# A decode-attention kernel: both output projections moved behind the last V, score chunks of 64 keys, q broadcast from its transpose

## The chip, the core and the metric

The kernel runs on one core of one Trainium2 chip. The metric is device time in microseconds, from several executions per kernel, each compared with executions of the kernel before on the same chip. All executions quoted here are of the state "fast". A time is a median; a "ratio" is the mean time of one kernel's fast runs over that of the other's fast runs of the same rounds, so it is not quite the ratio of two medians. The profile's "span" is shorter than the time, by about 1.8 us in nearly all executions. The 95% interval of every ratio is about 0.0013 either way, 3.4 us; where the text reads a smaller difference, it rests on the ranges of four or five runs each, and the kernel before stays within 0.4 us from one set of rounds to the next (medians 2583.15 to 2583.55).

## The reference

Two independent problems, A and B, each with batch 8, one query token, model width 1024, 32 heads of 128, and a cache of 4096 keys:

```
q      = x @ wq                                # [8, 32, 1, 128]
p      = softmax(q . k_cache * 128**-0.5)      # over 4096 keys
o      = p @ v_cache
result = o (heads side by side) @ wo           # [8, 1, 1024]
output = concat(A's result, B's result)        # bf16
```

K and V of one problem are 256 MiB each. Everything is bf16 and each cached value is used once, so the work is loading.

## The kernel before

The heads are taken eight at a time: a tile is 8 heads of one batch entry, 16 partitions per head, 256 keys per partition, 64 KB a partition, 8.39 MB. There are 64 K tiles and 64 V tiles, plus wq and wo of A and B, 8.39 MB each. SBUF has three slots of this size; K tiles alternate between slots 0 and 1, V has slot 2. One SyncE queue issues the loads in program order, each as soon as the last user of its slot has finished.

```python
put("wq", 0, 1); put("k", 0); put("wq", 1, 2)
for n in range(NQ - 1):                       # NQ = 64
    early = ...                               # some K in two halves
    put("k", n + 1, ...)
    put("v", n, 2)
    for c in range(NC):
        if n == done_at(c, NC, HB, B) + 1:    # wo of A in mid-program, 3/4 of wo of B late
            put("wo", c)
            late[n + 2] = c
put("v", NQ - 1, cuts=...)                    # last V in four pieces,
put("wo_last", 0, 2)                          # last quarter of wo of B among them
```

wo of A is loaded with contiguous rows of 64 KB a partition. wo of B is laid out by head, so that most of it can be projected before the last heads are done; its rows are 2 KB:

```python
opT[(kind, n)] = dma(to[:, 0:cols].rearrange("p (h n) -> p h n", n=D),
    caches[-1][4][heads.start * Dh:heads.stop * Dh, :].rearrange("(h p) n -> p h n", p=128), key, [dep])
```

For each K tile, in chunks of CT = 32 keys a partition, VectorE multiplies K by q in place and folds the 128 products to 64; TensorE adds four groups with the identity matrix; VectorE reduces the 16 left. After a whole tile come the maximum, the exponential (ScalarE), the masked weights PM (VectorE), and PV: 64 matmuls on TensorE, run while the next K tile is being scored. The end of PV frees the V slot. q is broadcast to the partitions of its head by eight small matmuls per tile.

```python
v, v * qbc                                   # make_mul,  VectorE
v[:, :, 0:64] + v[:, :, 64:128]              # make_fold, VectorE
matmul(dst, ident, v[:, :, j, :]) x 4        # make_eacc, TensorE
tensor_reduce(s_sb[...], red_ps[...], add)   # make_red,  VectorE
```

A small recorder in the file (class `_Program`) collects the operations of each engine and places the semaphore waits; every operation is emitted as straight code.

## Time and profile before

| | before |
|---|---|
| time | 2583.62 us (2583.49 to 2583.98, 3 runs) |
| span of the profiled execution | 2580.7 us |
| loaded | 1107.32 MB |
| VectorE busy | 2221.8 us, 86% |

The first lines are from the page of the kernel before: the busy time of each engine (share of the span, number of instructions), the loads' rate in 40 equal slices, the DMA queues (packets, MB, share of the time of 16 engines), and the chain of waits followed back from the end.

```profile
PE 1219.7 (47%) x7768; PEld 374.6 (15%) x7768; DVE 2221.8 (86%) x1809; ACT 105.2 (4%) x273; POOL 5.7 (0%) x23
GB/s 422 437 426 435 435 431 431 436 429 435 433 430 435 434 430 426 435 435 433 428 430 427 435 430 434 436 426 435 434 430 428 432 436 428 429 411 434 427 429 369
q1 hardware_dynamic: 23920, 1107.32, 99.5%
q8 instruction: 60, 0.98, 0.2%
q14 instruction: 18, 0.15, 0.0%
DMA 51%; DVE 46%; PE 2%; issue 1%; SPq 0%; ACT 0%; DVEq 0%
```

The queue of the loads (q1) is busy 99.5% of the time of 16 engines, at 430 GB/s nearly throughout. The chain of waits gives VectorE 46%, but that is how a chain is counted that walks through whatever released a load. A transfer that was released early and then stands behind another in the queue has not been delayed by its release: V is issued 8.1 us (median) before the last part of the load ahead of it lands.

Next, groups of instructions by line (operation, tiles and shapes, count, busy us, mean ns, idle time before and what ended it):

```profile
L305 DVE TENSOR_TENSOR ring<-ring,qbc 128x4096 bf16<-128x4096 bf16 x512 | 1169.0, 2283 | 327.0 <-DMA ring<-in_A_k_cache_dram 164.3
L310 DVE TENSOR_TENSOR ring<-ring 128x2048 bf16<-128x2048 bf16 x512 | 618.2, 1207 | 0.1
L327 DVE TENSOR_REDUCE s_sb<-red 128x32 f32<-128x512 f32 x512 | 348.3, 680 | 1.4 <-PE red L319 1.4
```

The multiply (L305) waits 327 us for K: VectorE is ahead of the loads. The table by stretch shows where the loads are slower than usual (stretch, length, busy us and instructions of PE, weight loads, VectorE, ScalarE, GpSimd, then TensorE's clock, DMA share, GB/s):

```profile
40.00:2280.00 2240.00, 1070.87 (x6720) 325.58 (x6720) 1975.59 (x1601) 87.66 (x233) 0.00 (x0) 0.60 1.00 432
2280.00:2340.00 60.00, 22.18 (x205) 8.17 (x206) 35.65 (x31) 1.48 (x4) 0.00 (x0) 0.61 0.99 405
2540.00:2575.00 35.00, 23.21 (x172) 9.77 (x172) 25.27 (x23) 1.20 (x3) 0.00 (x0) 0.63 0.89 371
```

The end of the chain of waits, in order of time (start, us, what):

```profile
2575.37 0.61 ACT accS L367
2576.02 0.28 PE o L384 x4
2576.39 0.45 DVE on_sb L420
2576.88 1.08 PE proj L439 x32
2577.98 0.42 DVE orow L447
```

After the last piece of V, the copy, the extraction of heads, the normalisation, a quarter of the projection and the store follow one another: about 6 us that nothing hides.

### The profile page before, as it was taken

The numbers are of one execution on the slowest core, as the hardware profiler recorded it, in microseconds if no ns is written. First come the engines' busy times: TensorE is split into PE (matmuls) and PEld (weight loads), VectorE is DVE, ScalarE is ACT, GpSimd is POOL, SyncE is SP. The second block draws the span as 40 slices with busy tenths as digits, with TensorE's granted clock in tenths as the row PEclk, the third lists the DMA queues.
The fourth block names the chain that finished last, engine by engine and source line by source line (L and its number), as shares of the span: only waits on it lengthen the run. The fifth ranks groups of instructions, "written<-read, shape, count | busy, mean of one in ns | idle before, by whom it ended". The sixth has DMA issues, their size and how long they took to land.

```text
span 2580.7 us, 17905 instructions
## 1 busy us (share of the span) xinstructions
PE 1219.7 (47%) x7768; PEld 374.6 (15%) x7768; DVE 2221.8 (86%) x1809; ACT 105.2 (4%) x273; POOL 5.7 (0%) x23
## 2 busy tenths in 40 slices
PE   2454454453554454454553445445345445453445
PEld 0111111111111111111111111111112111110112
DVE  3898898898898898898895889889889889887897
ACT  1100000000000000000000000000000000000000
POOL 0000000000000000000000000000000000000000
PEclk7665655655656655656655566565565565565656
DMA  9999999999999999999999999999999999999998
GB/s 422 437 426 435 435 431 431 436 429 435 433 430 435 434 430 426 435 435 433 428 430 427 435 430 434 436 426 435 434 430 428 432 436 428 429 411 434 427 429 369
DMA packets 24094, 1108.50 MB, mean 430 GB/s; under 512 B 2304, under 2 KB 2368, under 8 KB 6480
## 3 DMA queue, kind: packets, MB, share of 16 engines
q1 hardware_dynamic: 23920, 1107.32, 99.5%
q8 instruction: 60, 0.98, 0.2%
q14 instruction: 18, 0.15, 0.0%
q10 hardware_dynamic: 96, 0.05, 0.0%
HBM read 1107.33 MB, written 0.03 MB: 429 GB/s over the span
## 4 chain that ended last, share of the span: by engine, by line
DMA 51%; DVE 46%; PE 2%; issue 1%; SPq 0%; ACT 0%; DVEq 0%
DMA ring<-in_A_k_cache_dram 26%; DMA ring<-in_B_k_cache_dram 24%; DVE ring L305 24%; DVE ring L310 12%; DVE s_sb L327 6%; DVE PM L347 3%; PE red L319 2%; DVE rmax L333 1%; DMA ring<-in_B_v_cache_dram 1%; DVE rtmp L335 0%; DVE ngm L338 0%; PE pv L359 0%; SPq L158 0%; DVE rl L407 0%; DVE on_sb L414 0%
## 5 line engine op out<-in xcount | busy, mean ns | idle before, releaser
L319 PE MATMUL red<-ring,ident 128*128 128x512 bf16 x2048 | 836.5, 554 | 1321.2 <-DVE ring L310 1320.9
L305 DVE TENSOR_TENSOR ring<-ring,qbc 128x4096 bf16<-128x4096 bf16 x512 | 1169.0, 2283 | 327.0 <-DMA ring<-in_A_k_cache_dram 164.3
L310 DVE TENSOR_TENSOR ring<-ring 128x2048 bf16<-128x2048 bf16 x512 | 618.2, 1207 | 0.1
L319 PEld LDWEIGHTS red<-ring,ident 128*128 128x128 bf16 x2048 | 202.4, 120 | 1859.4 <-DVE ring L310 1590.8
L327 DVE TENSOR_REDUCE s_sb<-red 128x32 f32<-128x512 f32 x512 | 348.3, 680 | 1.4 <-PE red L319 1.4
L359 PE MATMUL pv<-ring,PM 128*32 128x512 bf16 x4096 | 320.2, 468 | 1.3 <-DMA ring<-in_B_v_cache_dram 1.3
L347 DVE TENSOR_TENSOR PM<-pe,own_h 128x2048 bf16<-128x2048 bf16 x64 | 146.2, 2284 | 0.7 <-ACT pe L341 0.7
L359 PEld LDWEIGHTS pv<-ring,PM 128*32 128x32 bf16 x4096 | 113.2, 113 | 216.1 <-issue 164.3
L341 ACT ACTIVATE pe<-s_sb,ngm 128x256 bf16<-128x256 f32 x64 | 32.5, 508 | 1008.0 <-DVE ngm L338 1008.0
L367 ACT ACTIVATE accS<-pv 128x512 bf16<-128x512 f32 x64 | 38.2, 597 | 846.0 <-PE pv L359 846.0
L295 ACT ACTIVATE qbc<-misc 128x128 bf16<-128x128 f32 x64 | 17.8, 278 | 580.6 <-PE misc L290 580.6
L333 DVE TENSOR_REDUCE rmax<-s_sb 128x1 f32<-128x256 f32 x64 | 26.9, 420 | 2.2
L290 PE MATMUL misc<-q_sb,selb 8*32 8x128 bf16 x512 | 26.2, 295 | 1.5 <-ACT q_sb L278 1.5
L377 PE MATMUL o<-accS,E 128*32 128x32 bf16 x512 | 18.1, 177 | 0.0
L335 DVE TENSOR_SCALAR rtmp<-half,rmax 128x32 f32<-128x32 f32 x64 | 15.4, 241 | 2.2
L290 PEld LDWEIGHTS misc<-q_sb,selb 8*32 8x32 bf16 x512 | 9.2, 103 | 54.7 <-issue 54.7
L377 PEld LDWEIGHTS o<-accS,E 128*32 128x32 bf16 x512 | 14.8, 94 | 13.6 <-ACT accS L367 8.1
L439 PE MATMUL proj<-ring,on_sb 128*8 128x256 bf16 x256 | 12.1, 372 | 9.4 <-DMA ring<-in_A_wo_dram 5.8
L338 DVE TRANSPOSE_TENSOR_REDUCE ngm<-rtmp 128x1 f32<-128x32 f32 x64 | 13.5, 211 | 2.2
L399 PEld LDWEIGHTS o<-rsum,own_m 128*128 128x128 f32 x64 | 14.5, 333 | 4.4 <-ACT pe L341 3.3
L399 PE MATMUL o<-rsum,own_m 128*128 128x8 f32 x64 | 13.8, 355 | 2.4 <-ACT pe L341 2.4
L269 PE MATMUL o<-ring,xT 128*8 128x512 bf16 x64 | 6.8, 599 | 11.0 <-DMA ring<-in_A_wq_dram 11.0
(36 smaller groups left out, 71.2 us busy)
## 6 DMA issues: line engine op xcount, KB each, us to landing
ring<-in_B_k_cache_dram SPq DMA_DIRECT2D x6, 4096.0 KB, 36.0
ring<-in_B_wo_dram SPq DMA_DIRECT2D x1, 6144.0 KB, 36.9
ring<-in_B_v_cache_dram SPq DMA_DIRECT2D x1, 4096.0 KB, 31.8
ring<-in_B_v_cache_dram SPq DMA_DIRECT2D x1, 2048.0 KB, 36.4
ring<-in_B_wo_dram SPq DMA_DIRECT2D x1, 2048.0 KB, 13.9
ring<-in_B_v_cache_dram SPq DMA_DIRECT2D x2, 1024.0 KB, 15.0
ring<-in_A_k_cache_dram SPq DMA_DIRECT2D x32, 41.6
ring<-in_A_v_cache_dram SPq DMA_DIRECT2D x32, 27.5
```

Source lines behind the costliest of these rows:

```text
L290: x = e.matmul(misc[32 * g:32 * (g + 1), 0:Dh], selb[rows, b, i, :], q_sb[rows, c, j * Dh:(j + 1) * Dh], start=(i == 0), stop=(i == 1), ti ...
L305: opMul[s] = add("dve", lambda e: e.tensor_tensor(v, v, qbc[:, n % 2, :].unsqueeze(1).to_broadcast([128, CT, Dh]), ALU.mult), [opT[("k", n ...
L310: return add("dve", lambda e: e.tensor_tensor(v[:, :, 0:64], v[:, :, 0:64], v[:, :, 64:128], ALU.add), [opMul[s]])
L319: i = e.matmul(dst, ident[:], v[:, :, j, :], start=(j == 0), stop=(j == 3))
L327: opRed[s] = add("dve", lambda e: e.tensor_reduce(s_sb[:, n % 2, r * CT:(r + 1) * CT], red_ps[s % 4][:, :].rearrange("p (t w) -> p t w", w ...
L333: opRmax[n] = add("dve", lambda e: e.tensor_reduce(rmax[:], s_sb[:, n % 2, :], AX.X, ALU.max), [opRed[NR * n + NR - 1]])
L341: opExp[n] = add("act", lambda e: e.activation(pe[:], s_sb[:, n % 2, :], ACTF.Exp, bias=ngm[:, n % 2:n % 2 + 1], scale=scale, accum_out=rs ...
L347: opPM[n] = add("dve", lambda e: e.tensor_tensor(PM[:], pe[:].unsqueeze(2).to_broadcast([128, T, HQ]), own_h[:].unsqueeze(1).to_broadcast( ...
L359: i = e.matmul(pv_ps[32 * q:32 * (q + 1), :], PM[:, t:t + 4, :].rearrange("p t j -> p (t j)"), v[:, t * Dh:(t + 4) * Dh], start=(g == 0), ...
L367: opAcc[n] = add("act", lambda e: e.activation(accS[:], pv_ps[:], ACTF.Copy), [opPV[n], _at(opExt, n - 1)])
L377: x = e.matmul(o_ps[MB * hb:MB * (hb + 1), H * b:H * (b + 1)], E[:, i, PH - 1 - u:PH - 1 - u + MB], accS[:, i * 128 + H * u:i * 128 + H * ...
L399: x = e.matmul(o_ps[:, HQ * B * HB + B * (HQ * hb + j):HQ * B * HB + B * (HQ * hb + j + 1)], own_m[:, j, 0:1].to_broadcast([128, 128]), rs ...
```

## The change

Intent: put everything that depends on the last heads behind loads that are still running. Both wo are loaded last, in contiguous rows, so PV, extraction and normalisation of the last tile happen while wo flows in; only the last small piece of wo is followed by exposed work. For that, the results of both problems must be kept until the end, which takes SBUF room; q is therefore kept transposed (1 KB a partition for all of A and B instead of 4) and broadcast by one matmul. The score chunks are doubled.

The diff, cut to its core:

```diff
-        CT = 32
+        CT = 64
-        red_ps = [ps(f"red{i}") for i in range(4)]
+        red_ps = [ps(f"red{i}", 16 * CT) for i in range(2)]
 ...
+        plan = [("wq", 0, 1), ("k", 0, 0), ("wq", 1, 2)]
         for n in range(NQ - 1):
+            plan.append(("k", n + 1, (n + 1) % 2))
+            plan.append(("v", n, 2))
+        plan += [("v", NQ - 1, NQ % 2), ("wo", 0, 2), ("wo", 1, (NQ - 1) % 2)]
 ...
+                    from_ = caches[n][4].rearrange("(p r) n -> p (r n)", r=H)
+                    for i, (r0, r1) in enumerate(wo_cuts if n == NC - 1 else ((0, H),)):
+                        opT[(kind, n, i)] = dma(to[:, r0 * D:r1 * D], from_[:, r0 * D:r1 * D], ...)
 ...   # wo_cuts: rows of 48, 12 and 4 KB a partition for wo of B
+        def make_qT(c):        # q transposed: 4 x (8 transposes on TensorE, 1 copy on VectorE)
+        def make_stage(n):     # ScalarE: a head's q on 16 columns
+        def make_qbc(n):       # one matmul with the identity, one ScalarE copy
-        def make_qbc(n):       # eight matmuls with a selector
 ...
+        LAG = 1                                      # was 2
+                if n == 0 and r == 1:                # was r in (5, 6) of eight chunks
+                    for c in range(1, NC):
+                        make_q(c)
+                        make_qT(c)
+                if r == 2 and n >= 1:
+                    make_pv(n - 1, 0, RG // 2)       # was chunk 5 of 0..7
+                if r == 3 and n >= 1:
+                    make_pv(n - 1, RG // 2, RG)      # was chunk 6
 ...
+LOOPS = {"pe": False, "dve": False}   # the recorder can also emit the tiles as a loop; off here
```

Each tile's output also gets a copy from PSUM to SBUF by ScalarE (`o_sb`), since PSUM is no longer where the results are collected.

## The prediction

> **What bounds the kernel now.** The loads. The page's DMA queue part shows 1107.32 MB with the 16 engines busy 99.5% of the span; the table by stretch, 432 GB/s from 40 to 2280 us. [...] One K tile plus one V tile (16.8 MB) take 38.9 us; VectorE works 34.7 us in that time (2221.8 us / 64) and then waits for K (327 us in all, list of groups). So VectorE (46% of the chain of waits) is off the critical path: the next V is issued about 8 us, the next K over 20 us, before the engines run dry (queue's timeline).
>
> Where the load stream is below 432 GB/s (table by stretch): 2280 to 2340 us at 405 (wo of B in 2 KB rows), about 3.7 us lost; 1300 to 1420 at 428 (wo of A), about 1; 2540 to 2575 at 371 (last V in pieces, last wo in 2 KB rows), about 5. After the last load lands (2574.1) come 6.6 us of PV, norm, projection and store.
>
> **What the change does.**
> - Bytes and steady state: unchanged, 38.9 us per tile pair.
> - 64-key chunks: the multiply goes from 2.20 us start to start to an estimated 4.33, the fold 1.13 to 2.20, the reduction 0.60 to 1.13. [...] Off the path: gain 0.
> - q broadcast: off the path.
> - wo last, in contiguous rows: the 2 KB-row losses go. Last V lands about 39 us before the end, so PV, extraction and norm hide behind wo. After the last load only some matmuls, a 0.42 us copy and the store remain: about 5 us, not 6.6. Gain: about 9 us of stream, 1.5 of tail.
> - PV of the previous tile now runs in chunks 2 and 3 of four; its end, which frees the V slot, comes about 34 us after K lands instead of 31. Slack 8 becomes 4 to 5.
> - Start: q of B is now projected at the second of four chunks, its transposes copied by VectorE in order. wq of B lands at 62.7 us, so VectorE, done with its second fold near 58, waits until about 74. PV(0) ends near 122 instead of 112. K(2) lands at 120.8; V(1) is issued only then: the engines idle an estimated 2 to 6 us, once.
>
> **Net.** Last load lands near 2569 us in the span, end near 2574, plus the 2.9 us between span and time: 2577 us, 80% range 2568 to 2587. Chance of faster by over 2%: 0.01; within 2%: 0.97; slower by over 2%: 0.02.
>
> **What would show it.** DMA share still about 99%; 432 GB/s in the middle and no dip at 2280 to 2340; one dip near 118 to 125 us; VectorE busy about 2170 us; waits of the multiply on K above 380 us; K issue of tile 2 near 91 us instead of 76; some 5 us after the last landing.
>
> **What would make it wrong.** A stall that repeats: if the V slot comes free later than 38.9 us after K lands, every tile pays. The start stall may be 0 or 15 us. A stream rate 0.3% different is 8 us. Slow small pieces of wo (12 KB and 4 KB rows) would shrink the end gain.

The last load near 2569 us, 5 us to the end and 2.9 us from span to time make 2577 us. The estimated 4.33, 2.20 and 1.13 us come to twice the 2.20, 1.13 and 0.60 us of 32 keys, less some 0.06 to 0.07 us. The trace of the kernel before shows such a difference: start to start, a multiply of 4096 elements takes 2.202 us and two folds of half that size 2.264.

## The result

The changed kernel takes 2575.77 us (2575.00 to 2577.44, 4 runs) against 2583.55 us (4 runs by then): 7.8 us less, ratio 0.9972 (95% interval 0.9958 to 0.9986). The prediction said 2577. The profiled execution happens to be the slowest of the four (span 2575.7 us; the other three have 2573.3 to 2574.7), and the profiled one of before is about 1 us shorter than usual (2580.7; most others 2581.0 to 2582.2, five of the 36 later ones at 2580.3 to 2580.9), so the two profiles show 5.0 of the 7.8 us.

The same parts of the page for the changed kernel:

```profile
PE 1118.2 (43%) x7712; PEld 395.3 (15%) x7712; DVE 2170.7 (84%) x1043; ACT 130.0 (5%) x401; POOL 2.5 (0%) x14
GB/s 423 424 434 430 435 434 429 437 430 434 432 432 437 427 436 430 433 434 432 428 435 432 435 427 434 431 433 433 433 431 431 432 437 431 431 431 431 432 435 370
q1 hardware_dynamic: 19360, 1107.32, 99.6%
q8 instruction: 60, 0.98, 0.2%
q14 instruction: 13, 0.11, 0.0%
DMA 52%; DVE 42%; PE 5%; issue 1%; another core or an unknown queue 0%; ACT 0%; SPq 0%
```

The chain of waits keeps nearly the same shares. The groups that answer to those of before:

```profile
L316 DVE TENSOR_TENSOR ring<-ring,qbc 128x8192 bf16<-128x8192 bf16 x256 | 1132.0, 4422 | 314.0 <-DMA ring<-in_B_k_cache_dram 157.7
L321 DVE TENSOR_TENSOR ring<-ring 128x4096 bf16<-128x4096 bf16 x256 | 582.7, 2276 | 0.0
L339 DVE TENSOR_REDUCE s_sb<-red 128x64 f32<-128x1024 f32 x256 | 312.3, 1220 | 3.7 <-PE red L331 3.7
```

VectorE does the same work in 766 fewer instructions and 51 us less, about 67 ns for each instruction saved. The multiply of 64 keys starts 4.33 us before the next instruction (98.86 to 103.19 in the timeline), against 2.20 us for 32 keys in the kernel before: 0.07 us less than two of them. Fold and reduction save as much (medians of start to start: 2.198 us against two of 1.132, 1.134 against two of 0.601). So part of an instruction's time, here about 0.07 us, did not grow with its size. None of this time is on the critical path; e10 tests that.

The table by stretch:

```profile
40.00:2280.00 2240.00, 978.23 (x6466) 341.03 (x6467) 1942.46 (x922) 110.30 (x349) 0.00 (x0) 0.68 1.00 432
2280.00:2340.00 60.00, 29.32 (x218) 10.57 (x218) 50.33 (x23) 2.92 (x9) 0.00 (x0) 0.70 0.99 427
2540.00:2560.00 20.00, 7.82 (x184) 4.83 (x176) 1.92 (x3) 0.78 (x2) 0.00 (x0) 0.74 0.99 423
2560.00:2575.00 15.00, 5.17 (x128) 3.50 (x128) 0.42 (x1) 0.00 (x0) 0.00 (x0) 0.77 0.48 201
```

The dip at 2280 us is gone, but the loads still fade out over the last 15 us. The end of the chain of waits:

```profile
2531.15 36.53 DMA ring<-in_B_wo_dram
2567.82 4.78 PE proj L415 x116
2572.63 0.42 PE proj L415 x8
2573.08 0.42 DVE orow L419
```

After the last landing (2572.6) only 8 matmuls, one copy and the store remain: 3.1 us instead of 6.0.

And the start. First the timeline of VectorE in the changed kernel, where it stands from 58 to 70 us and then waits again between the four copies of q transposed; then the queue's timeline in both kernels, before first:

```profile
55.73 2.28 DVE L321 TENSOR_TENSOR ring<-ring 128x4096 bf16<-128x4096 bf16 x1
70.44 0.19 DVE L291 COPY qT<-misc 128x64 bf16<-128x64 bf16 x1 [12.43 <-PE misc L287]
72.59 0.19 DVE L291 COPY qT<-misc 128x64 bf16<-128x64 bf16 x1 [0.54 <-PE misc L287]
72.70 4.42 DVE L316 TENSOR_TENSOR ring<-ring,qbc 128x8192 bf16<-128x8192 bf16 x1
```

```profile
76.06 0.33 SPq L158 DMA_DIRECT2D ring<-in_A_k_cache_dram  x1
112.20 0.33 SPq L158 DMA_DIRECT2D ring<-in_A_v_cache_dram  x1
```

```profile
91.80 0.33 SPq L198 DMA_DIRECT2D ring<-in_A_k_cache_dram  x1
118.12 0.33 SPq L198 DMA_DIRECT2D ring<-in_A_v_cache_dram  x1
```

K of tile 2 is issued at 91.8 us instead of 76.1 (predicted: 91), V of tile 1 at 118.1 instead of 112.2 (predicted: 122). That V lands 2.34 us later than before (142.54 against 140.20).

### A finer look: sixteen landings per load

An average of GB/s hides that a load lands in parts. The page counts 16 engines, a tile is 128 packets of 64 KB, its rows, and the trace has 16 increments of the semaphore per load. I read an increment as one engine's part, 8 of the rows; the pace below fits that. What waits for the load starts after the last part: in the changed kernel the last matmuls start at 2572.63 us, 0.04 us after it. Worked out from the increments, for the last load of each kernel (us from the start of the span):

```
                 first part   last part   spread   end of span - last part
before             2571.87     2574.66     2.79      6.02
changed            2565.44     2572.59     7.15      3.13
```

In the changed kernel some engines are through 7 us before others (1.9 us in the first tiles). The stream of the *last* engine is what the time follows. Taking the last landing of each tile and the time between two of them shows a remarkably even pace: 19.345 us per tile, which is eight packets of 64 KB at 2.42 us. Now and then one interval is longer; call that a slip. From the first load to the last, the last landing falls 17.8 us behind this pace in the kernel before and 15.7 us in the changed one (time between the two landings, less 131 tiles at 19.345 us). In the changed kernel eight slips are of 1.5 us or more: V of tile 1 (2.2 us) and seven of 1.5 to 1.7 us that come about every 350 us. Each of the seven intervals has a packet of q8 in it: instructions, counted by the page on the same 16 engines (0.2% of their time). A packet of q8 comes about every 43 us, so that alone says little; but the seven are exactly every eighth packet, and at the packets between them the last landing keeps its pace.

What one packet costs can be read from the changed kernel's trace. At 58 of the 60 packets of q8 (16 KB, 0.93 to 1.11 us) a load packet of 64 KB starts within 0.02 us of the instruction packet's end and takes about 2.91 us instead of 2.42. Read as packets of one engine, it loses both: 1.56 us in the median. At the 13 packets of q14 (8 KB, 0.31 to 0.33 us) the load packet behind takes 3.07 us in the median, and the loss is 0.98 us. These are the sizes of the slips. The trace does not name the engine of a packet, so that each eighth packet falls on the engine that ends last is a reading, which e7 and e9 test.

### The profile page after: what moved, and what is told of

Same layout as the page of the kernel before. It is cut to its first block, busy times and chain, and to the rows that moved or that the text cites. A ratio compares the mean times of both kernels' runs of the same rounds, so it can differ in the third digit from the quotient of the medians.

```text
span 2575.7 us, 17138 instructions
## 1 busy us (share of the span) xinstructions
PE 1118.2 (43%) x7712; PEld 395.3 (15%) x7712; DVE 2170.7 (84%) x1043; ACT 130.0 (5%) x401; POOL 2.5 (0%) x14
## 4 chain that ended last, share of the span: by engine, by line
DMA 52%; DVE 42%; PE 5%; issue 1%; another core or an unknown queue 0%; ACT 0%; SPq 0%
DMA ring<-in_B_k_cache_dram 25%; DMA ring<-in_A_k_cache_dram 25%; DVE ring L316 22%; DVE ring L321 11%; DVE s_sb L339 4%; PE red L331 4%; DVE PM L356 3%; DMA ring<-in_B_wo_dram 1%; DVE rmax L345 1%; DVE rtmp L346 0%; DVE ngm L349 0%; PE proj L415 0%; PE o L271 0%; PE pv L271 0%
## 5 line engine op out<-in xcount | busy, mean ns | idle before, releaser
L316 DVE TENSOR_TENSOR ring<-ring,qbc 128x8192 bf16<-128x8192 bf16 x256 | 1132.0, 4422 | 314.0 <-DMA ring<-in_B_k_cache_dram 157.7
L331 PE MATMUL red<-ring,ident 128*128 128x512 bf16 x2048 | 783.0, 552 | 1395.2 <-DVE ring L321 1395.2
L321 DVE TENSOR_TENSOR ring<-ring 128x4096 bf16<-128x4096 bf16 x256 | 582.7, 2276 | 0.0
L331 PEld LDWEIGHTS red<-ring,ident 128*128 128x128 bf16 x2048 | 239.8, 128 | 1847.6 <-DVE ring L321 1497.4
L339 DVE TENSOR_REDUCE s_sb<-red 128x64 f32<-128x1024 f32 x256 | 312.3, 1220 | 3.7 <-PE red L331 3.7
L368 PE MATMUL pv<-ring,PM 128*32 128x512 bf16 x4096 | 272.9, 413 | 4.6 <-DVE PM L356 4.6
L305 ACT ACTIVATE qbc<-misc 128x128 bf16<-128x128 f32 x64 | 17.8, 278 | 1075.0 <-PE misc L303 1075.0
L386 PEld LDWEIGHTS o<-accS,E 128*32 128x32 bf16 x1024 | 31.3, 100 | 48.9 <-issue 47.7
L386 PE MATMUL o<-accS,E 128*32 128x32 bf16 x1024 | 38.1, 185 | 0.7 <-ACT accS L376 0.7
L391 ACT ACTIVATE o_sb<-o 32x32 f32<-32x32 f32 x64 | 11.9, 186 | 446.0 <-PE o L386 445.4
L298 ACT ACTIVATE qst<-qT 128x128 bf16<-128x128 bf16 x64 | 18.7, 293 | 1.0 <-DVE qT L291 1.0
L349 DVE TRANSPOSE_TENSOR_REDUCE ngm<-rtmp 128x1 f32<-128x32 f32 x64 | 13.5, 212 | 2.2
```

The source lines that it names most:

```text
L298: opSt[n] = add("act", lambda e: e.activation(qst[:, n % 2, :].rearrange("p (j m) -> p j m", m=MP), from_.unsqueeze(2).to_broadcast([128, ...
L305: opQbc[n] = add("act", lambda e: e.activation(qbc[:, n % 2, :], misc[:, 0:Dh], ACTF.Copy), [opQb[n], _at(opMul, NR * (n - 2) + NR - 1)])
L316: opMul[s] = add("dve", lambda e: e.tensor_tensor(v, v, qbc[:, n % 2, :].unsqueeze(1).to_broadcast([128, CT, Dh]), ALU.mult), [opT[("k", n ...
L321: return add("dve", lambda e: e.tensor_tensor(v[:, :, 0:64], v[:, :, 0:64], v[:, :, 64:128], ALU.add), [opMul[s]])
L331: i = e.matmul(dst, ident[:], v[:, g, :, j, :], start=(j == 0), stop=(j == 3))
L339: opRed[s] = add("dve", lambda e: e.tensor_reduce(s_sb[:, n % 2, r * CT:(r + 1) * CT], red_ps[s % 2][:, :].rearrange("p (t w) -> p t w", w ...
```

## The experiments

Theory 1, the one of the prediction, is that the load stream sets the time and that the gain comes from the end of the program. Its rival, theory 2, is that VectorE's shorter program (46% of the chain of waits before) gives it. Theory F, formed from the finer look, is that the instructions fetched over the load engines set the pace of the last engine. A first set undoes parts of the change. The diffs are abridged, partly in words.

### e1: chunks of 32 keys again

```diff
-    CT = 64
+    CT = 32
-  red_ps ... for i in range(2)      # and opRed s - 2, LAG = 1
+  red_ps ... for i in range(4)      # and opRed s - 4, LAG = 2
-  q of B at chunk 1, PV at chunks 2 and 3 of 4
+  q of B at chunk 2, PV at chunks 4 and 6 of 8
```

> The changed kernel with the chunks of scores put back to 32 keys (four PSUM buffers, reductions two chunks behind), everything else as changed. Theory 1 (the load stream sets the time; the gain came from the end of the program, wo last): VectorE busy goes back up to about 2220 us, the waits of the multiply on K shrink by about 50 us, the time stays at 2575.8 within 2 us. Theory 2 (VectorE's chain, 46% of the chain of waits, gave the gain): the time goes back towards 2583, at least 4 us of the 7.8 are lost.

Measured: 2581.07 us (2580.42 to 2581.99), ratio to before 0.9993; 5.3 us slower than the changed kernel. Theory 1 as I held it is wrong here: the chunks matter. V of tile 1 was issued at 121.4 us and landed at 144.47, 1.9 us after the changed kernel's: part of the loss is at the start. The rest was not explained by theory 2 either, as e10 shows below.

### e2: q by the selector again

```diff
-  make_qT, make_stage, make_qbc (one matmul)
+  make_qbc (eight matmuls with selb), q_sb in a tile of its own
-  o_sb FP32; on_sb, orow tiles of their own
+  o_sb BF16; on_sb, orow laid over s_sb      # else SBUF is too small
```

> The changed kernel with q broadcast as before, by eight matmuls with a selector from q in rows (o_sb in bf16 and two late tiles laid over the scores' buffer, because there is no room otherwise). Theory 1: the steady state does not notice; the copies of q transposed no longer hold VectorE at the start, but the projection of q still holds the reduction matmuls of the second chunk, so the start stall may shrink by up to 2 us: 2574 to 2577. Theory 2: slower than the changed kernel by 2 us or more, because PE and ACT work per tile is back as before.

Measured: 2575.39 us (2575.01 to 2576.01), ratio 0.9970. The broadcast of q is worth nothing in time; it makes room. (Built with the other tiles as they were, this kernel did not fit into SBUF: the build stopped at o_sb, which needs 2048 B a partition where 1472 were left.)

### e3: only wo last

e1 and e2 together.

> The changed kernel with both of the other parts put back: chunks of 32 keys and q by the selector. What remains is wo loaded last in contiguous rows. Theory 1: the whole gain remains, 2574 to 2577 us. Theory 2: most of the gain is gone, 2580 us or more.

Measured: 2577.81 us (2576.88 to 2578.02), ratio 0.9978, between what the two theories expected. So wo last alone gives 5.3 of the 7.8 us, and doubling the chunks on top of it 2.4 (e3 against e2). With the broadcast from the transpose, chunks of 32 lose 3.3 us more (e1 against e3): there the late q of B holds the second V until 121.4 us, against 113.6 in e3, and its landing slips by 4.3 us, against none in e3. No run moves q alone in e1.

### e4: q of B projected later

```diff
-                if n == 0 and r == 1:
+                if n == 0 and r == 3:
```

> The changed kernel with q of B projected and transposed at the fourth chunk of the first tile instead of the second. Theory 1: VectorE no longer waits from 58 to 72 us for the copies of q transposed, the second K is issued near 82 us instead of 91.8, V of tile 1 before 116 us instead of at 118.1, and the load stream has no gap near 118 us: about 2 us faster, 2573.5 to 2575. If the start stall cost nothing: 2575.8 as before.

Measured: 2575.85 us (2575.48 to 2576.14), ratio 0.9972. K of tile 2 was issued at 80.6 us and V of tile 1 at 112.0, and the latter landed 2.5 us earlier than in the changed kernel (140.09), as expected; the time did not move. A stall that happens early was lost in something that came later.

### e5 and e6: the rows of wo of B

e5 gives the kernel before contiguous rows; e6 gives the changed kernel rows of 2 KB. Both have a wrong result for B on purpose.

```diff
-  to[...].rearrange("p (h n) -> p h n"), wo[heads].rearrange("(h p) n -> p h n", p=128)
+  to[...],                               wo.rearrange("(p r) n -> p (r n)")[:, heads * D]     # e5; e6 the reverse
```

> The kernel before with wo of B loaded in contiguous rows of 48 and 16 KB instead of rows of 2 KB, at the same places in the order of loads; the half of the output for B is wrong on purpose. My prediction put the rows' cost at about 3.7 us in the middle and part of 5 at the end. Theory 1 read by the average rate: 3 to 5 us faster than before, 2579 to 2581. Theory 1 read by the queue that lands last (the dip let the queues that ran ahead wait for the late one): 2 to 3 us faster, 2581 to 2582. If the rows cost nothing: 2583.6.

> The changed kernel with wo of B loaded last in rows of 2 KB instead of 48, 12 and 4 KB; wrong on purpose in the half for B. If rows of 2 KB cost what they seemed to in the kernel before (8.4 MB at about 400 instead of 432 GB/s): 1.5 to 3 us slower than the changed kernel, 2577.5 to 2579. If not: 2575.8.

Measured: e5 2581.70 us (2581.26 to 2582.72), ratio 0.9994, 1.7 us less than before (the 95% interval of the ratio, 0.9981 to 1.0008, includes 1; the ranges of the runs do not meet); e6 2578.31 us (2577.65 to 2578.72), ratio 0.9980, 2.5 us more than the changed kernel. In e6 the three loads of wo of B take 22.4 us from last landing to last landing, against 19.5 in the changed kernel: that is the cost of the rows where nothing else limits.

e5 shows that contiguous rows alone do not remove the dip at 2280 us: the stretch still moves at 405 GB/s (columns as in the tables by stretch above):

```profile
2310.00:2312.00 2.00, 0.75 (x3) 0.36 (x4) 1.19 (x2) 0.00 (x0) 0.00 (x0) 0.90 0.06 25
2280.00:2340.00 60.00, 23.78 (x204) 8.50 (x204) 34.94 (x30) 1.48 (x4) 0.00 (x0) 0.59 0.95 405
```

The engines run dry at 2310 us, because the next load had not been issued. wo takes one of the two K slots, so K of tile 58 has to wait for the slot of K of tile 57, until that tile is scored. From the chain of waits of the kernel before:

```profile
2311.55 1.05 PE red L319 x4
2312.62 23.10 DMA ring<-in_B_k_cache_dram
```

In the kernel before, the first engine is through with wo at 2310.55 us, 2.1 us before that issue. It is the one load there that is issued after an engine has run dry. By the landing of this K, e5 is no earlier than before (2336.12 against 2335.72): its gain comes after it. In the kernel before, wo falls 1.3 us behind the even pace (its rows) and this K 0.9; in e5 wo keeps the pace and the K alone falls 3.0 us behind. With wo last, neither slip is there. e5's 1.7 us is therefore no clean measure of the rows. After the pause the landings of the kernel before are close together again: the spread of the 16 falls from 5.45 us (V of tile 55, at 2261 us) to 1.82 (K of tile 58, at 2336 us).

### e7 and e8: TensorE's program as a loop

The recorder of the changed kernel can emit the steady tiles as a loop of 30 rounds of two tiles, with the semaphore values of the waits computed from the round. That is meant to take TensorE's instructions out of the fetch; whether it does is read from the packets of q8 below.

```diff
-LOOPS = {"pe": False, "dve": False}
+LOOPS = {"pe": True, "dve": False}        # e8: and "n == 0 and r == 3" of e4
```

> The changed kernel with TensorE's program for tiles 3 to 62 written as a loop of 30 rounds. In the trace of the changed kernel 60 packets of 16 KB of instructions go over the same 16 queue engines, each makes one 64 KB load packet take 2.9 us instead of 2.42, and the last load lands on its 16 parts over 7.2 us. Theory F (fetching TensorE's instructions delays some of the 16 engines, and the last of them sets the end): the fetch packets fall to a few, the spread of the last landing falls to 4 us or less, and the time falls by 3 to 5 us to 2571 to 2573. Rival (the spread has other causes): fetch falls, the time stays at 2575.8 within 1 us, or rises through the register arithmetic of the waits.

> The changed kernel with both: q of B at the fourth chunk and TensorE's tiles as a loop. If the two costs are separate, their gains add: 2569 to 2572 us. If both only remove the same slack at the start, no more than the better of the two.

Measured: e7 2572.38 us (2571.46 to 2573.68), ratio 0.9958; e8 2572.42 us (2571.57 to 2572.94), ratio 0.9957. The time fell by 3.4 us, as theory F expected, and again the later q added nothing. The spread of the last landing did not fall to 4 us, though: it is 6.3 us in e7. The queues in e7:

```profile
q1 hardware_dynamic: 19360, 1107.32, 99.7%
q8 instruction: 9, 0.15, 0.0%
q14 instruction: 13, 0.11, 0.0%
```

The packets of q8 went from 60 to 9, so most of q8 was TensorE's instructions, and 9 are too few for the loop's body to have been fetched again in each of its 30 rounds. The last landing falls 9.7 us behind the even pace instead of 15.7. What was left of slips over 0.3 us (7.6 us together; 13.5 in the changed kernel) were seven of about 0.97 us (one of them 0.48), each beside a packet of q14, plus one of 1.35 at V of tile 1.

### e9: both loops

```diff
-LOOPS = {"pe": False, "dve": False}
+LOOPS = {"pe": True, "dve": True}         # and "n == 0 and r == 3"
```

> The changed kernel with q of B at the fourth chunk and both TensorE's and VectorE's tiles 3 to 62 as loops (the kernel of e8 with VectorE's loop added). In e7 the last of the 16 landings still slips seven times by 0.97 us, each time at one of the 8 KB instruction packets (13 in that trace). Theory F (the fetch of instructions over the load engines is what is left above 19.345 us a tile): these packets fall to a few, the last load lands 4 to 6 us earlier than in e8, time 2566 to 2569. If those packets are not VectorE's, or if only TensorE's fetch cost time: 2572.4. If the register arithmetic of the waits slows VectorE enough to delay V: above 2573.

Measured: 2565.53 us (2564.76 to 2565.64), ratio 0.9931: 6.9 us less than e8, 10.2 less than the changed kernel, 18.0 less than before, and the result is correct. That is more than the 2566 to 2569 expected. The spread of the last landing is 2.14 us, the sum of the slips over 0.3 us is 0.8 us, and the last landing falls 2.8 us behind the even pace. From the page:

```profile
PE 1122.0 (44%) x7712; PEld 394.9 (15%) x7712; DVE 2170.6 (85%) x1043; ACT 129.9 (5%) x401; POOL 2.6 (0%) x14
GB/s 425 427 438 430 437 431 436 432 436 432 435 433 435 433 435 433 435 433 435 433 435 433 434 434 434 434 434 434 434 433 435 433 435 432 436 432 436 432 435 387
q8 instruction: 9, 0.15, 0.0%
q14 instruction: 5, 0.04, 0.0%
```

The work of VectorE and TensorE is what it was; the packets of q14 fell from 13 to 5, so most of q14 was VectorE's instructions; and the row of GB/s is smooth.

### e10: both loops, chunks of 32

```diff
-    CT = 64          # the kernel of e9
+    CT = 32          # with the edits of e1, and q of B at chunk 6 of 8
```

> The kernel of e9 with chunks of 32 keys. In straight code chunks of 32 cost 2.4 us (e3 against e2). Theory F: they cost it because 768 more VectorE instructions mean more instruction packets (19 instead of 13) on an engine that is already last; in a loop the packets are gone, so the time equals e9's within 1 us although VectorE is busy 50 us longer. Theory V (VectorE's longer work frees V later and the stream waits): at least 2 us slower than e9, as in straight code.

Measured: 2565.87 us (2564.77 to 2566.31), ratio 0.9932. From the page:

```profile
PE 1172.3 (46%) x7712; PEld 362.8 (14%) x7712; DVE 2222.3 (87%) x1811; ACT 129.8 (5%) x401; POOL 2.5 (0%) x14
q14 instruction: 6, 0.05, 0.0%
```

VectorE is busy 52 us longer than in e9 with 768 more instructions, and the time is the same within 0.4 us. This separates the two things that longer chunks change. VectorE's time is off the path; the number of its instructions was on it, through the fetch. In straight code e3 had 19 packets of q14 and fell 15.1 us behind the even pace, e2 13 packets and 13.2 us:

```profile
q14 instruction: 19, 0.16, 0.0%
```

That line is e3's page. The difference, 1.9 us, is close to the 2.4 us between their times.

### e11: both loops, q of B early

```diff
-                if n == 0 and r == 3:    # the kernel of e9
+                if n == 0 and r == 1:
```

> The kernel of e9 with q of B back at the second chunk, so that the start stall is back. In straight code moving q away landed V of tile 1 2.1 us earlier and changed the time by 0.1 us (e4). If that is because the engine that ends last is one that instruction packets delay later, so that engines ahead of it lose nothing by waiting once, then without those packets the stall costs its 1 to 2 us: 2566.5 to 2567.7. If the stall costs nothing in itself: 2565.5 as e9.

Measured: 2565.78 us, but with a wide range (2565.11 to 2568.01; e9: 2564.76 to 2565.64), ratio 0.9935. Three of five runs equal those of e9, two are 1.5 to 2.5 us slower. In the profiled one, a slow one, V of tile 1 lands 0.9 us later than in e9, and 1.5 us more are lost at K of tile 4, with an instruction packet of q8 in that interval; 1.5 us is what one such packet costs an engine. This is inconclusive: the start stall costs between 0 and 2.5 us, and whether that packet falls on the engine that ends last may decide, which one profile cannot show.

### Where the 7.8 us came from

| step | time, us | difference |
|---|---|---|
| before | 2583.2 to 2583.6 | |
| wo last, contiguous rows (e3) | 2577.81 | -5.3 (against 2583.15 of the same rounds) |
| and chunks of 64 (e2) | 2575.39 | -2.4 |
| and q from its transpose (changed) | 2575.77 | +0.4, within the scatter |
| and both loops, q of B later (e9) | 2565.53 | -10.2 |

The first step can be followed in the profiles of the kernel before and of e3, whose spans differ by 5.6 us. The tail from last landing to end is 2.9 us shorter (6.0 to 3.1), and the last landing comes 2.7 us earlier. Of these 2.7, wo of B in mid-program and the K behind it give 2.1 (rows and late issue together, and contiguous rows alone would not have won it, as e5 shows), and the last quarter of wo, in rows of 2 KB before, 0.6. Over the rest of the program both fall 15.1 us behind the even pace. Around wo of A in mid-program there is a slip of 1.0 us in the kernel before (K of tile 33), but e3 has the same one at the same place, beside a packet of q14, so moving wo of A gained nothing there.

## Why the prediction was right or wrong, point by point

- **"What bounds the kernel now. The loads."** Right over the program as a whole, and e10 against e9 shows that 52 us more of VectorE's time cost nothing in the looped kernel. The exception in the kernel before is K of tile 58: there the loads waited for scores (2.1 us behind the even pace, with wo before it).
- **"64-key chunks: ... Off the path: gain 0."** The durations were right to 0.01 us (4.33, 2.20, 1.13), the conclusion wrong: the chunks gave 2.4 us (e3 against e2). The reasoning looked at VectorE's time only. The instructions are traffic too: 19 packets of q14 with chunks of 32 (e3), 13 with 64 (e2), and one costs its engine 0.98 us in the changed kernel's trace.
- **"q broadcast: off the path."** Right for its steady work (e2: 0.4 us). Its real role, room in SBUF for keeping both results, was not seen; e2 did not build without it until other tiles were packed.
- **"Gain: about 9 us of stream."** The wrong size, and in part the wrong cause. It summed the shortfall of an average rate. The landing that counts came 2.1 us earlier in the two profiles, the start stall of 2.3 us included. It put the dip at 2280 us (3.7 us) down to rows of 2 KB; e5 has contiguous rows there and the same 405 GB/s, because the K behind wo is issued too late; wo and this K cost 2.1 us together. The fading of the rate at the end (371 GB/s before, 201 in the last 15 us after) goes with the spread of the 16 engines, which the change did not shrink: 2.8 us before, 7.2 after.
- **"1.5 of tail."** Undersized: 2.9 us in the two profiles (6.0 to 3.1).
- **"the engines idle an estimated 2 to 6 us, once."** The mechanism and the moments were right (K of tile 2 at 91.8 us, V of tile 1 late, 401 GB/s between 120 and 130 us), and V of tile 1 landed 2.34 us later than before. The time lost by it was nothing in straight code (e4): removing it changed 0.1 us. My reading, consistent with e2, e4 and e8 but not settled by e11, is that an engine that is ahead can afford to wait, when another will be delayed later and end last.
- **"waits of the multiply on K above 380 us"** Wrong, 314. VectorE's idle time did rise, from 359 to 405 us (span less busy time), but 33 us of it now stand before the copies of q transposed, and the longest waits for K of before (31 and 27 us) are gone.
- **"2577 us."** 2575.77 measured. It is right by terms that offset one another, so in part by luck: too much from the stream, too much lost at the start, too little from the tail, and nothing from the chunks. The span was forecast at 2574 and measured at 2573.3 to 2575.7; the 2.9 us that were added for the step from span to time, taken from the profile of the kernel before, were 1.7.
- **"A stall that repeats"** did not come: V is issued in time in every later tile, as the even pace of 19.345 us between last landings shows. Nor did the slack shrink to "4 to 5" as forecast: V is issued 8.6 us (median) before the last part of the load ahead of it lands, against 8.1 before.

## What to carry to other kernels

When a kernel is bound by loads, follow the last of the 16 landings of each load, not the average GB/s. Before a dip is put down to the shape of a load, check that the next load was issued before the engines ran dry. Then ask what else those engines carry. In this long straight program the instructions are part of the traffic (60 packets of 16 KB and 13 of 8 KB in the changed kernel), and fewer of them (larger chunks, or better a loop) gained what shortening the compute did not: the loops gave 10 us where the whole change gave 8.
